# Linear attention feeding two expert stages: queries transposed beside the keys in float32, keys times values summed over pairs of units one iteration later

## The chip, the cores and the metric

The kernel runs on one core of one Trainium2 chip. The metric is the device time of one execution in microseconds; the lower the better. TensorE (PE, with its weight loads shown as PEld), VectorE (DVE), ScalarE (ACT), GpSimd (POOL) and SyncE's queue of transfers (SP) each run their own instructions in order and wait for one another through semaphores.

## The reference, cut to what matters

Batch 4, 8 heads, 576 positions, head size 64, 128 features; everything is float32.

```
phi(x): proj = x @ w_phi;  proj -= max(|proj|, over features)
        return concat(exp(proj), exp(-proj))                # 256 features
q_p, k_p = phi(q), phi(k)
kv  = sum_s k_p[s, f] * v[s, d]          # per head: 256 x 64
z   = sum_s k_p[s, f]
out = (q_p @ kv) / (q_p @ z + 1e-6)
x   = out with the heads side by side    # 2304 rows of 512
x   = top-2 mixture of 8 experts: relu(x @ w1[e]) @ w2[e], gated
y   = relu(x @ w_in)^2 @ w_out
```

## The kernel before

**Stages.** An attention loop, then eight experts of at most 640 rows each, then the dense layer. Rows go to their experts through a table in DRAM (`xg_d`) by indirect transfers that GpSimd issues (`r_5`). If an expert gets more than 640 rows, a branch at the end of the program (`tc.If(most > CAP)`) computes everything again from a copy of the attention output in `x_d`; with these inputs it is not taken, but the copy is written each time (L580, L584).

**The attention loop.** It runs n = 0 to 37. A unit is one of nine per batch: unit 0 holds the 64 tail positions of all heads, and units 1 to 8 hold 512 positions each, for keys two heads in two halves (so a pair of units makes a pair of heads), for queries one head. The order of instructions is written by hand; each step of unit u is issued in the iteration that its lag names, so in one iteration several units are at different steps. On TensorE an iteration runs, in this order:

- `k_a(n+1)`: two float32 transposes of keys into bank Tk; ACT writes the rounded high part (`kth`), DVE the low part (`ktl`).
- `q_a(n-1)`: four transposes of the query tile in float32r, high and low parts side by side, into bank Tq; ACT copies the 512 columns out (`qtr`). The high and low parts were made from the loaded tile in SBUF by `q_a0` (ACT L84, DVE L85, tile `qhl`).
- `k_b(n)`: six matmuls of key features into bank M0 or M1, then DVE's maximum (L374) and subtraction (L377).
- `q_b(n-2)`: two matmuls over 128 rows (64 of the high part, 64 of the low) and 512 columns into bank P; ACT copies them out (L473), and GpSimd takes the maximum over partitions (L475).
- `k_d(n-2)` after each second unit: eight small matmuls (`gmat`, `sel`) into Tk and a copy to `kvc`.
- `k_c(n-1)`: keys times values into bank KV, two 64-column tiles of the array at a time, then sums of the keys in four 32-column tiles (`ones`); for the first unit of a pair also the tail positions (`kpt`, from 64 rows); after the second, DVE copies the bank to `kvz` (L421), for `k_d`.
- `q_d(n-5)`: 16 matmul instructions of queries times `kvc` into N0 or N1; DVE normalizes them (`norm`) one iteration later.

Between these steps a table (`at`, `do`) hands out the rest: routing of each batch (`r_0` to `r_6`, `q_tail`), clearing of `xg_d` (`clear`), and loading and splitting the first experts' weights (`w_load`, `w_conv`). Transfers wait in SP's one queue in the order of issue.

Of the kernel before, what the change touches and what calls it, by code (L numbers as in the profile page):

```python
# [20 lines left out]
WST = 4  # L21

# [8 lines left out]
def kernel(  # L31
# [45 lines left out]
    def bank(tag, shape, dt=FT):  # L77
        return psum.tile(shape, dt, tag=tag, name=tag)
# [18 lines left out]
    LQ = [(0, 0), (0, 1), (0, 2), (1, 0), (0, 3), (1, 1), (1, 2), (1, 3)]  # L97
# [50 lines left out]
    def x_load(pt):  # L148
        e, j0, j1 = parts[pt]
        if e == E - 1:  # L150
            j1 = NJ
        src = xg_d[e * CAP:e * CAP + CAP].rearrange("(j p) d -> p j d", p=128)
        if pt == 1:
            for j in range(j0, j1):
                t = stage.tile([128, DM], FT, name="xs", tag="wstage", bufs=WST)
                nc.sync.dma_start(t, src[:, j])
                XG[pt, j] = t
        else:
            t = x_tile(pt, [128, JA if pt == 0 else NJ, DM], FT, "xg", ("qhlt", 1))
            nc.sync.dma_start(t[:, :j1], src[:, :j1])  # L160
            for j in range(j1):
                XG[pt, j] = t[:, j]

    def x_t(pt, j):
        e = parts[pt][0]
        if pt not in XT:
            n = RA if pt == 0 else CAP
            XT[pt] = (x_tile(pt, [128, DC, n], FR, "xth", ("kp", 2)), x_tile(pt, [128, DC, n], FR, "xtl", ("kp", 2)))
# [58 lines left out]
    with ExitStack() as actx:  # L227
# [28 lines left out]
        def load_tails(b):  # L256
            t = ap_.tile([TL, H, D], FT, name="ktt", tag="ktt", bufs=2)
# [7 lines left out]
            t = ap_.tile([128, 4, D], FT, name="vtt", tag="vtt", bufs=2)  # L265
            for s in range(2):
                nc.sync.dma_start(t[s * 64:(s + 1) * 64],
# [13 lines left out]
        identr = ap_.tile([128, 128], FR, name="identr", tag="identr")  # L281
# [13 lines left out]

        wf = ap_.tile([128, 128], FT, name="wf", tag="wf")
# [10 lines left out]
        jp = ap_.tile([128, 128], I32, name="jp", tag="jp")  # L307
        nc.gpsimd.iota(jp, pattern=[[1, 128]], base=0, channel_multiplier=-1)
        nc.vector.tensor_scalar(ident, jp, 0.0, None, op0=OP.is_equal)
        nc.scalar.activation(identr, ident, AF.Copy)  # L310
# [34 lines left out]
        def k_a(u):  # L345
            b, i = divmod(u, 9)
            t = bank("Tk", [128, 256])
            if i == 0:
                for p in range(4):
                    c = (p % 2 * 2 + p // 2) * 64  # L350
                    nc.tensor.transpose(t[:, c:c + 64],
                                        KTT[b][:, 2 * p:2 * p + 2, :].rearrange("p h d -> p (h d)"), ident[:64, :64])
            else:
                p, f = divmod(i - 1, 2)
                for h in range(2):
                    nc.tensor.transpose(t[:, h * 128:h * 128 + 128],  # L356
                                        KT[b, p][:, h, 2 * f:2 * f + 2, :].rearrange("p r d -> p (r d)"), ident)
            hi = ap_.tile([128, 256], FR, name="kth", tag="kth", bufs=2)
            lo = ap_.tile([128, 256], FR, name="ktl", tag="ktl", bufs=2)
            hi_lo(hi, lo, t)  # L360
            KH[u] = (hi, lo)

        def k_b(u):
# [15 lines left out]
            if i == 0:  # L379
                kp = ap_.tile([128, 4, 2, 128], FT, name="kpt", tag="kpt", bufs=1)  # L380
# [11 lines left out]
        def k_c(u):  # L392
            b, i = divmod(u, 9)
            if i == 0:
                return
            p, f = divmod(i - 1, 2)
            if f == 0:
                KVB[b, p] = bank("KV", [128, 512])
            t = KVB[b, p]
            kp = KP.pop(u).rearrange("p (h r) a f -> p r h (a f)", h=2)  # L400
            for r in range(2):
                for h in range(2):
                    mm(t[h * 64:h * 64 + 64, :256], VT[b, p][:, h, 2 * f + r, :], kp[:, r, h],
                       f == 0 and r == 0, f == 1 and r == 1)
            for h in range(2):
                for r in range(2):
                    g = 32 * (2 * h + r)
                    mm(t[g:g + 32, 256:], ones32, kp[:, r, h], False, f == 1)
            if f == 0:
                rows = slice((p // 2) * 64, (p // 2) * 64 + 64)  # L410
                kt = KPT[b].rearrange("p (r h) a f -> p r h a f", h=2)
                for h in range(2):
                    mm(t[h * 64:h * 64 + 64, :256], VTT[b][rows, (p % 2) * 2 + h, :],
                       kt[rows, p % 2, h].rearrange("p a f -> p (a f)"), False, False)
                for h in range(2):
                    for a in range(2):
                        g = 32 * (2 * h + a)
                        mm(t[g:g + 32, 256 + a * 128:384 + a * 128], ones32[rows], kt[rows, p % 2, h, a], False, False)
            else:
                kvz = ap_.tile([128, 512], FT, name="kvz", tag="kvz", bufs=1)  # L420
                nc.vector.tensor_copy(kvz, t)  # L421
                KVZ[b, p] = kvz

        def k_d(u):
            b, i = divmod(u, 9)
# [5 lines left out]
            t = bank("Tk", [128, 2, 162])  # L431
# [7 lines left out]
        QHL, QTR, PS, QP, QPT, X, XTL, LL = {}, {}, {}, {}, {}, {}, {}, {}  # L439

        def q_a0(u):
            b, i = divmod(u, 9)
            if i == 0:
                s = ap_.tile([TL, H, 2, D], FR, name="qhlt", tag="qhlt", bufs=1)
                hi_lo(s[:, :, 0, :], s[:, :, 1, :], QTT[b])
            else:
                s = ap_.tile([128, R, 2, D], FR, name="qhl", tag="qhl", bufs=2)
                hi_lo(s[:, :, 0, :], s[:, :, 1, :], QT[b, i - 1])
            QHL[u] = s

        def q_a(u):
            b, i = divmod(u, 9)
            t = bank("Tq", [128, 512], FR)
            s = QHL.pop(u)
            if i == 0:
                for h in range(H):
                    nc.tensor.transpose(t[:, h * 64:h * 64 + 64],
                                        s[:, h].rearrange("p a d -> p (a d)"), identr[:64, :64])
            else:
                for r in range(R):  # L460
                    nc.tensor.transpose(t[:, r * 128:r * 128 + 128],  # L461
                                        s[:, r].rearrange("p a d -> p (a d)"), identr)
            o = ap_.tile([128, 512], FR, name="qtr", tag="qtr", bufs=2)
            nc.scalar.activation(o, t.bitcast(FT), AF.Copy)
            QTR[u] = o

        def q_b(u):
            t = bank("P", [128, 512])
            o = QTR.pop(u)
            mm(t, wsh, o, True, False)  # L470
            mm(t, wsl, o, False, True)
            ps = ap_.tile([128, 512], FT, name="ps", tag="ps", bufs=3)
            nc.scalar.activation(ps, t, AF.Copy)  # L473
            mx = ap_.tile([128, 512], FT, name="qmx", tag="qmx", bufs=3)
# [39 lines left out]
        def q_d(u):  # L514
# [9 lines left out]
            for j in range(R):  # L524
                h = i - 1 if b < B - 1 else 2 * hp + j // 2
                for a in range(2):
                    mm(t[:, j], qp[:, a, j * 128:j * 128 + 128],
# [8 lines left out]
        def q_tail(b1, n, tag):  # L536
# [3 lines left out]
            for hh in range(4):  # L540
                h = 4 * n + hh
                for a in range(2):
                    for s in range(2):
                        mm(t[s * 64:s * 64 + 64, hh], QPT[b1 - 1 + s][:, a, h * 64:h * 64 + 64],
# [717 lines left out]
```

## Time and profile before

| what | value |
|---|---|
| median of 3 runs | 1131.83 us (1131.06 to 1132.64) |
| profiled execution | 1142.34 us, its span 1140.6 us |
| busy PE, DVE, ACT, POOL | 97%, 56%, 43%, 35% of the span |
| granted TensorE clock, mean | 0.987 |
| moved by DMA | 142.51 MB |

The profile is of one execution, longer by 10.5 us than the median of the runs. The attention loop takes its first 240 us or so; a busy share there is an average over iterations with different limits, and matmuls are pipelined, so what a matmul costs is read from the start of one group to the start of the next rather than from its own duration.

### The profile page before, as it was taken

The numbers are of one execution on the slowest core, as the hardware profiler recorded it, in microseconds if no ns is written. First come the engines' busy times: TensorE is split into PE (matmuls) and PEld (weight loads), VectorE is DVE, ScalarE is ACT, GpSimd is POOL, SyncE is SP. The second block draws the span as 40 slices with busy tenths as digits, with TensorE's granted clock in tenths as the row PEclk, the third lists the DMA queues.
The fourth block names the chain that finished last, engine by engine and source line by source line (L and its number), as shares of the span: only waits on it lengthen the run. The fifth ranks groups of instructions, "written<-read, shape, count | busy, mean of one in ns | idle before, by whom it ended". The sixth has DMA issues, their size and how long they took to land.

```text
span 1140.6 us, 17665 instructions
## 1 busy us (share of the span) xinstructions
PE 1101.5 (97%) x6588; PEld 935.0 (82%) x6588; DVE 642.7 (56%) x1247; ACT 493.8 (43%) x1025; POOL 396.8 (35%) x374
## 2 busy tenths in 40 slices
PE   7999889989999999999999999999999999999996
PEld 4676667678889999999999988888898888888885
DVE  6778778775148687878777774343343333333222
ACT  5767567641453535444445354443233232222221
POOL 3333342743545454545454545553010010000000
PEclk9999999998999999999999999999999999999998
DMA  5768352614646555555555555332112011001001
GB/s 133 223 178 263 89 168 65 208 75 173 224 142 199 180 193 183 193 178 189 179 194 180 196 182 164 122 109 74 37 39 55 19 38 56 19 1 37 1 1 40
DMA packets 106366, 142.51 MB, mean 125 GB/s; under 512 B 17570, under 2 KB 59682, under 8 KB 105762
## 3 DMA queue, kind: packets, MB, share of 16 engines
q1 hardware_dynamic: 100514, 122.44, 33.9%
q0 software_dynamic: 5760, 18.88, 5.1%
q8 instruction: 54, 0.88, 0.3%
q14 instruction: 38, 0.31, 0.1%
HBM read 92.97 MB, written 48.31 MB: 124 GB/s over the span
## 4 chain that ended last, share of the span: by engine, by line
PE 86%; DVE 6%; DMA 2%; issue 2%; ACT 1%; another core or an unknown queue 1%; POOL 1%; SPq 0%; POOLq 0%
PE M L81 38%; PE N L81 16%; PE KV L81 12%; PE P L81 9%; PE Tq L81 8%; DVE qhl L85 1%; PE Tk L81 1%; PE Tq L461 1%; PE M L173 1%; DMA wstage<-in_moe_w_dram 1%; DVE kmx L374 1%; PE Tk L995 1%; PE Tk L173 1%; PE Tk L356 1%
## 5 line engine op out<-in xcount | busy, mean ns | idle before, releaser
L1016 DVE TENSOR_TENSOR r<-M,r 128x512 f32<-128x512 f32 (+1 forms) x80 | 51.0, 638 | 245.1 <-ACT h2h L1015 242.3
L1012 ACT ACTIVATE r<-M 128x512 f32<-128x512 f32 (+1 forms) x80 | 44.4, 555 | 247.7 <-PE M L81 245.5
L202 ACT ACTIVATE hh<-M 128x320 fp32r<-128x320 f32 (+2 forms) x128 | 50.8, 437 | 227.7 <-PE M L81 220.6
L199 DVE SCALAR_TENSOR_TENSOR hl<-M,hh 128x320 fp32r<-128x320 f32 (+2 forms) x128 | 58.1, 486 | 114.7 <-ACT hh L202 113.4
L475 POOL PARTITION_ALL_REDUCE qmx<-ps x36 | 69.9, 1942 | 137.0 <-ACT ps L473 132.7
L977 POOL DMA_INDIRECT ya<-y_d,yrows x18 | 17.9, 997 | 187.2 <-PE Tk L995 112.5
L81 PEld LDWEIGHTS N<-kvc,qp 128*128 128x128 f32 x512 | 62.1, 197 | 17.5 <-issue 11.9
L81 PE MATMUL N<-kvc,qp 128*128 128x81 f32 x512 | 67.0, 284 | 9.5 <-issue 4.2
L1017 DVE TENSOR_TENSOR h2l<-r,h2h 128x512 fp32r<-128x512 f32 (+1 forms) x80 | 57.7, 721 | 7.3 <-DVE r L1016 0.5
L1015 ACT ACTIVATE h2h<-r 128x512 fp32r<-128x512 f32 (+1 forms) x80 | 47.1, 589 | 2.6
L81 PE MATMUL M<-x,w30h 128*128 128x512 f32 (+1 forms) x160 | 45.9, 371 | 0.0
L81 PE MATMUL M<-x,w20h 128*128 128x512 f32 (+1 forms) x160 | 45.7, 370 | 0.0
L81 PE MATMUL M<-x,w10h 128*128 128x512 f32 (+1 forms) x160 | 45.7, 370 | 0.0
L81 PE MATMUL M<-x,w00h 128*128 128x512 f32 (+1 forms) x160 | 45.4, 368 | 0.0
L128 POOL TENSOR_TENSOR w30l<-wstage,w30h 128x512 fp32r<-128x512 f32 x20 | 27.4, 1370 | 49.9 <-ACT w30h L127 47.4
L128 POOL TENSOR_TENSOR w20l<-wstage,w20h 128x512 fp32r<-128x512 f32 x20 | 28.0, 1399 | 45.0 <-ACT w20h L127 29.4
L740 POOL DMA_INDIRECT xg_d<-x,slots x32 | 31.9, 997 | 21.7 <-DVE slots L701 11.8
L85 DVE TENSOR_TENSOR qhl<-qt,qhl 128x256 fp32r<-128x256 f32 x32 | 37.0, 1156 | 0.4 <-ACT qhl L84 0.4
L128 POOL TENSOR_TENSOR w10l<-wstage,w10h 128x512 fp32r<-128x512 f32 x16 | 22.3, 1394 | 40.6 <-ACT w10h L127 36.8
L947 POOL TENSOR_TENSOR wd<-wd 128x256 f32<-128x256 f32 x32 | 23.7, 741 | 36.0 <-DVE wd L943 31.7
L947 POOL TENSOR_TENSOR wx<-wx 128x256 f32<-128x256 f32 x32 | 23.7, 740 | 35.1 <-DVE wx L943 31.6
L952 DVE SCALAR_TENSOR_TENSOR wd<-wd 128x256 f32<-128x256 f32 x32 | 35.1, 1096 | 1.1
(439 smaller groups left out, 3465.0 us busy)
## 6 DMA issues: line engine op xcount, KB each, us to landing
wstage<-in_moe_w_dram SPq DMA_DIRECT2D x128, 256.0 KB
xg_d<-zero SPq DMA_DIRECT2D x8, 1280.0 KB
y_d<-y SPq DMA_DIRECT2D x40, 256.0 KB
xg<-xg_d SPq DMA_DIRECT2D x7, 1280.0 KB
wide<-in_moe_w_in_dram SPq DMA_DIRECT2D x32, 256.0 KB
wide<-in_moe_w_out_dram SPq DMA_DIRECT2D x32, 256.0 KB
kt<-in_k_dram SPq DMA_DIRECT2D x16, 256.0 KB
vt<-in_v_dram SPq DMA_DIRECT2D x16, 256.0 KB
```

The costliest lines, as they stand in the source:

```text
L81: nc.tensor.matmul(o, l, r, start=start, stop=stop, skip_group_check=True)
L85: nc.vector.tensor_sub(lo, src, hi.bitcast(FT))
L128: (nc.gpsimd if n >= 2 else nc.vector).tensor_sub(lo[:, c], src, hi[:, c].bitcast(FT))
L199: nc.vector.scalar_tensor_tensor(hl[:, c0:c1], o, 0.0, hh[:, c0:c1].bitcast(FT), op0=OP.max, op1=OP.subtract)
L202: nc.scalar.activation(hh[:, c[1]:c[2]], c[0], AF.Relu)
L475: nc.gpsimd.partition_all_reduce(mx, ps, 128, bass.bass_isa.ReduceOp.absmax)
L947: nc.gpsimd.tensor_mul(part, part, exp)
L952: nc.vector.scalar_tensor_tensor(exp, ok, TINY * TINY, exp, op0=OP.is_ge, op1=OP.mult)
L1012: nc.scalar.activation(r[:, :n], t[:, :n], AF.Relu)
L1015: nc.scalar.activation(hh[:, :n], r[:, :n], AF.Square)
L1016: nc.vector.tensor_mul(r[:, :n], t[:, :n], r[:, :n])
L1017: nc.vector.tensor_sub(hl[:, :n], r[:, :n], hh[:, :n].bitcast(FT))
```

## The change

- `k_a`, `q_a0` and `q_a` become `kq_a`: the keys of unit n+1 and the queries of unit n-1 are transposed in float32 (two transposes each) into one 512-column bank, and one ACT and one DVE instruction make high and low parts of both. The tile `qhl`, the copy `qtr` and the identity `identr` go.
- `q_b`: two heads lie one above the other in the rows, so each product is taken from 64 rows: three products (high by high, high by low, low by high), each as two matmuls of 256 columns, one on the upper 64 rows into bank Tq, one on the lower 64 into bank P. The two banks become one tile, `pair`; the experts' and the dense layer's accumulators Tq and P are slices of it as well.
- `k_c` issues the values' products of both units of a pair at once. `k_c2`, an iteration later, adds the tail positions and all sums of the keys, and the bank is then copied to `kvz` by ACT, not DVE. The tails' values lie in 128 rows padded with zeros (`vtp`), the ones in `onesp`, so these matmuls use 128 rows.
- `k_d` follows an iteration later, after `k_c2`, into M0 or M1. The order of the last batch's query units changes (`LQ`).
- More buffers for `kp` and `kpt`; the weights' loads are issued two iterations earlier; the first tiles of expert 0 take their memory from `kp`.
- `x_d` is no longer written in the loop; the branch at the end gathers it from the table.

```
+PAIR = ["Tq", "P"]
...
+    pair = psum.tile([128, 2, 512], FT, tag="pair", name="pair")
+
+    def bank(tag, shape):
+        if tag not in PAIR:
+            return psum.tile(shape, FT, tag=tag, name=tag)
...
+        return pair[:, PAIR.index(tag), :n].rearrange(
...
-    LQ = [(0, 0), (0, 1), (0, 2), (1, 0), (0, 3), (1, 1), (1, 2), (1, 3)]
+    LQ = [(0, 0), (0, 1), (1, 0), (0, 2), (0, 3), (1, 1), (1, 2), (1, 3)]
...
-            t = x_tile(pt, [128, JA if pt == 0 else NJ, DM], FT, "xg", ("qhlt", 1))
+            t = x_tile(pt, [128, JA if pt == 0 else NJ, DM], FT, "xg", ("kp", 4))
...
+        vtp = [ap_.tile([128, H, D], FT, name="vtp", tag=f"vtp{i}") for i in range(2)]
+        onesp = ap_.tile([128, 2, 32], FT, name="onesp", tag="onesp")
+        for t in vtp:
+            nc.gpsimd.memset(t, 0.0)
...
-        def k_a(u):
...
+        def kq_a(n):
+            uk, uq = n + 1, n - QO + 1
...
+            t = bank("Tk", [128, 512])
...
+                    for h in range(2):
+                        nc.tensor.transpose(t[:, h * 128:h * 128 + 128],
+                                            KT[b, p][:, h, 2 * f:2 * f + 2, :].rearrange("p r d -> p (r d)"), ident)
...
+                    for f in range(2):
+                        nc.tensor.transpose(t[:, 256 + f * 128:384 + f * 128],
+                                            QT[b, i - 1][:, 2 * f:2 * f + 2, :].rearrange("p r d -> p (r d)"), ident)
+            hi = ap_.tile([128, 512], FR, name="kth", tag="kth", bufs=2)
+            lo = ap_.tile([128, 512], FR, name="ktl", tag="ktl", bufs=2)
+            c = slice(0 if has_k else 256, 512 if has_q else 256)
+            hi_lo(hi[:, c], lo[:, c], t[:, c])
...
-                kp = ap_.tile([128, 4, 2, 128], FT, name="kp", tag="kp", bufs=2)
+                kp = ap_.tile([128, 4, 2, 128], FT, name="kp", tag="kp", bufs=4)
...
         def k_c(u):
             b, i = divmod(u, 9)
+            if i == 0 or i % 2:
+                return
...
+            for f in range(2):
+                for r in range(2):
+                    for h in range(2):
+                        mm(t[h * 64:h * 64 + 64, :256], VT[b, p][:, h, 2 * f + r, :], kps[f][:, r, h],
+                           f == 0 and r == 0, False)
+
+        def k_c2(u):
...
+            for h in range(2):
+                mm(t[h * 64:h * 64 + 64, :256], VTT[b][:, 2 * p + h], kt[:, h].rearrange("p a f -> p (a f)"), False, True)
+            for f in range(2):
+                for h in range(2):
+                    for r in range(2):
+                        g = 32 * (2 * h + r)
+                        mm(t[g:g + 32, 256:], ones32, kps[f][:, r, h], False, f == 1)
             for h in range(2):
...
+                for a in range(2):
+                    g = 32 * (2 * h + a)
+                    mm(t[g:g + 32, 256 + a * 128:384 + a * 128], onesp[:, p // 2], kt[:, h, a], False, True)
+            kvz = ap_.tile([128, 512], FT, name="kvz", tag="kvz", bufs=1)
+            nc.scalar.activation(kvz, t, AF.Copy)
...
-            t = bank("Tk", [128, 2, 162])
+            t = bank(f"M{(u + 1 - 1) % 2}", [128, 2, 162])
...
-        def q_a0(u):
...
-        def q_a(u):
...
         def q_b(u):
-            t = bank("P", [128, 512])
-            o = QTR.pop(u)
-            mm(t, wsh, o, True, False)
-            mm(t, wsl, o, False, True)
+            hi, lo = QH.pop(u)
+            for i, (w, x) in enumerate(((wsh, hi), (wsl, hi), (wsh, lo))):
+                for s in range(2):
+                    rows = slice(s * 64, s * 64 + 64)
+                    mm(pair[:, s, :256], w[rows], x[rows, 256:], i == 0, i == 2)
...
-            if r + G >= R:
-                nc.sync.dma_start(_ap(x_d, b * S * DM, [[R * DM, 128], [1, R * DM]]), X[b].rearrange("p r d -> p (r d)"))
...
-            at(6 + 2 * m, 9, w_load, n, i, c)
+            at(4 + 2 * m, 9, w_load, n, i, c)
...
-            if n + 1 < NU:
-                k_a(n + 1)
...
+            kq_a(n)
             if n < NU:
                 k_b(n)
...
-            if 0 <= n - 2 < NU:
-                k_d(n - 2)
...
             if 0 <= n - 1 < NU:
                 k_c(n - 1)
+
+            if n <= NU:
+                k_c2(n - 2 if n < NU else n - 1)
+            if n <= NU + 1:
+                k_d(n - 3 if n <= NU else n - 2)
             if 0 <= n - QC < NU:
                 q_d(n - QC)
```

## Rows read from the trace of the kernel before

**Rows 1.** Busy us by stretch: PE, PEld, DVE, ACT, POOL, then granted clock, DMA share, GB/s.

```profile
80.00:90.00 10.00, 7.50 (x67) 5.34 (x68) 5.60 (x14) 5.23 (x12) 2.19 (x2) 0.98 0.96 234
...
130.00:140.00 10.00, 7.41 (x70) 5.82 (x68) 6.46 (x15) 4.50 (x9) 4.77 (x5) 0.87 0.44 131
140.00:150.00 10.00, 8.71 (x84) 6.88 (x85) 5.68 (x20) 4.40 (x9) 3.73 (x5) 0.79 0.09 32
```

**Rows 2.** The same view, a stretch of the experts.

```profile
340.00:380.00 40.00, 40.00 (x230) 36.13 (x229) 30.92 (x50) 16.16 (x39) 19.79 (x17) 1.00 0.53 173
```

**Rows 3.** The chain that ended last, two of its pieces: start, us, what.

```profile
74.84 9.40 DMA wstage<-in_moe_w_dram
...
145.99 1.32 DVE qhl L85
```

**Rows 4.** TensorE's timeline, an undisturbed stretch: start, us, what, count.

```profile
40.89 0.38 PE L356 MATMUL Tk<-ident,kt 128*128 128x128 f32 x2
...
41.40 0.35 PE L81 MATMUL M<-wbh,kth 128*128 128x256 f32 x1
...
42.19 0.40 PE L81 MATMUL P<-qtr,wsh 128*128 128x512 f32 x1
...
42.76 1.08 PE L81 MATMUL KV<-kp,vt 128*64 128x256 f32 x8
43.77 0.64 PE L81 MATMUL KV<-kp,ones 128*32 128x256 f32 x8
44.34 2.01 PE L81 MATMUL N<-kvc,qp 128*128 128x81 f32 x16
46.28 0.46 PE L351 MATMUL Tk<-ident,ktt 64*128 64x64 f32 x4
46.67 0.54 PE L461 MATMUL Tq<-identr,qhl 128*128 128x128 f32 x4
...
49.28 1.08 PE L81 MATMUL KV<-kp,vt 128*64 128x256 f32 x8
...
50.86 0.65 PE L81 MATMUL KV<-kpt,vtt 64*64 64x256 f32 x4
51.44 0.42 PE L81 MATMUL KV<-kpt,ones 64*32 64x128 f32 x8
51.79 2.01 PE L81 MATMUL N<-kvc,qp 128*128 128x81 f32 x16
53.64 0.38 PE L356 MATMUL Tk<-ident,kt 128*128 128x128 f32 x2
...
59.25 0.83 PE L457 MATMUL Tq<-identr,qhlt 64*128 64x64 f32 x8
60.01 0.38 PE L81 MATMUL M<-wbh,kth 128*128 128x256 f32 x1
```

**Rows 5.** TensorE's timeline, where later batches begin, and the second batch's long wait.

```profile
110.45 0.38 PE L356 MATMUL Tk<-ident,kt 128*128 128x128 f32 x2
...
129.40 1.34 PE L81 MATMUL N<-kvc,qpt 128*64 128x81 f32 x32
...
136.83 3.09 PE L81 MATMUL N<-kvc,qp 128*128 128x81 f32 x16 [2.59 <-ACT qp L493]
...
178.70 0.38 PE L356 MATMUL Tk<-ident,kt 128*128 128x128 f32 x2
...
234.47 0.52 PE L461 MATMUL Tq<-identr,qhl 128*128 128x128 f32 x4
```

**Rows 6.** Groups by line over the span: busy us, mean ns, idle before.

```profile
L85 DVE TENSOR_TENSOR qhl<-qt,qhl 128x256 fp32r<-128x256 f32 x32 | 37.0, 1156 | 0.4 <-ACT qhl L84 0.4
...
L464 ACT ACTIVATE qtr<-Tq 128x512 fp32r<-128x512 f32 x36 | 21.4, 596 | 3.7 <-PE Tq L461 2.3 <-PE Tq L457 1.1
...
L85 DVE TENSOR_TENSOR xtl<-M,xth 128x512 fp32r<-128x512 f32 x24 | 16.6, 691 | 14.5 <-ACT xth L84 14.5
...
L421 DVE COPY kvz<-KV 128x512 f32<-128x512 f32 x16 | 10.9, 680 | 0.0
```

More of the change, by code (lines that the diff above doesn't have):

```diff
@@ L75 @@
     g_d = dram.tile([NT, E], FT, name="g_d")
-    def bank(tag, shape, dt=FT):
-        return psum.tile(shape, dt, tag=tag, name=tag)
+    pair = psum.tile([128, 2, 512], FT, tag="pair", name="pair")
+    def bank(tag, shape):
+        if tag not in PAIR:
+            return psum.tile(shape, FT, tag=tag, name=tag)
+        names = "abc"[:len(shape) - 1]
+        n = 1
+        for x in shape[1:]:
+            n *= x
+        return pair[:, PAIR.index(tag), :n].rearrange(
+            f"p ({' '.join(names)}) -> p {' '.join(names)}", **dict(zip(names, shape[1:])))
     def mm(o, l, r, start, stop):
@@ L343 @@
         KH, KP, KPT, KVB, KVZ, KVC, KE = {}, {}, {}, {}, {}, {}, []
-        def k_a(u):
[L346 to L361, printed above, removed]
+        def kq_a(n):
+            uk, uq = n + 1, n - QO + 1
+            has_k, has_q = uk < NU, 0 <= uq < NU
+            if not (has_k or has_q):
+                return
+            t = bank("Tk", [128, 512])
+            if has_k:
+                b, i = divmod(uk, 9)
+                if i == 0:
+                    for p in range(4):
+                        c = (p % 2 * 2 + p // 2) * 64
+                        nc.tensor.transpose(t[:, c:c + 64],
+                                            KTT[b][:, 2 * p:2 * p + 2, :].rearrange("p h d -> p (h d)"), ident[:64, :64])
+                else:
+                    p, f = divmod(i - 1, 2)
+                    for h in range(2):
+                        nc.tensor.transpose(t[:, h * 128:h * 128 + 128],
+                                            KT[b, p][:, h, 2 * f:2 * f + 2, :].rearrange("p r d -> p (r d)"), ident)
+            if has_q:
+                b, i = divmod(uq, 9)
+                if i == 0:
+                    for p in range(4):
+                        nc.tensor.transpose(t[:, 256 + p * 64:320 + p * 64],
+                                            QTT[b][:, 2 * p:2 * p + 2, :].rearrange("p h d -> p (h d)"), ident[:64, :64])
+                else:
+                    for f in range(2):
[5 more added lines that the diff above has]
+            hi_lo(hi[:, c], lo[:, c], t[:, c])
+            if has_k:
+                KH[uk] = (hi, lo)
+            if has_q:
+                QH[uq] = (hi, lo)
@@ L393, in k_c @@
             b, i = divmod(u, 9)
-            if i == 0:
+            if i == 0 or i % 2:
                 return
[L396 to L401, printed above, removed]
+            p = (i - 1) // 2
+            t = bank("KV", [128, 512])
+            kps = [KP.pop(u - 1 + f).rearrange("p (h r) a f -> p r h (a f)", h=2) for f in range(2)]
@@ L578, in r_0 @@
             yield
-            if r + G >= R:
-                nc.sync.dma_start(_ap(x_d, b * S * DM, [[R * DM, 128], [1, R * DM]]), X[b].rearrange("p r d -> p (r d)"))
-            if r + G > R:
-                for s in range(2):
-                    row = (b - 1 + s) * S + SM
-                    nc.sync.dma_start(x_d[row:row + TL], XTL[b][s * 64:s * 64 + 64])
         def r_1(g):
@@ L1185, in flip @@
                 return o
+            for b in range(B):
+                for r in range(R + b % 2):
+                    x = tile_([128, DM], "sx")
+                    nc.gpsimd.indirect_dma_start(
+                        out=x, out_offset=None, in_=xg_d,
+                        in_offset=bass.IndirectOffsetOnAxis(ap=slots[:, T0[b] + r, 0:1], axis=0))
+                    if r < R:
+                        nc.sync.dma_start(_ap(x_d, (b * S + r) * DM, [[R * DM, 128], [1, DM]]), x)
+                    else:
+                        for s in range(2):
+                            row = (b - 1 + s) * S + SM
+                            nc.sync.dma_start(x_d[row:row + TL], x[s * 64:s * 64 + 64])
             with tc.For_i(0, NT, 128) as row:
```

92 lines of the change are left out of this document (29 added, 63 removed).

## The prediction

> **What bounds it now.** I read the busy times by stretch first. From 340 us on TensorE is busy 40.00 us of 40 [rows 2] and the diff leaves that work as it is, so what can move is the attention loop. There TensorE is nearly always the busiest, but not full: 7.50 us of 10 from 80 us, 7.41 from 130, 8.71 from 140, and from 130 its granted clock is 0.87 and then 0.79 of full, which means part of these stretches ran at the lower of its two levels (1.2 against 2.4 GHz) [rows 1]. The chain of waits says what fills the holes: a 9.40 us transfer of weights before ScalarE's split of them, and VectorE's `qhl` [rows 3]. The reader should see two kinds of loss: instructions on TensorE that take long, and waits.
>
> The timeline of TensorE prices both [rows 4]. Starts, not durations: front of an iteration (six transposes, six key matmuls, two query matmuls) 42.76 − 40.89 = 1.87 us; a second-of-pair `k_c` 44.34 − 42.76 = 1.58; a first-of-pair one 51.79 − 49.28 = 2.51; the pair of iterations 53.64 − 40.89 = 12.75, of which 0.25 is the tail keys' transposes (46.67 − 46.28 = 0.39 against some 0.14). A batch without waits is four pairs, 4 × 12.5 = 50.0, a ninth front 1.87, and tails of 0.25 and about 0.4 (eight transposes take 60.01 − 59.25 = 0.76, four some 0.38): 52.5 us. The batches that begin at 53.64, 110.45 and 178.70 took 56.8, 68.2 and 55.8 us [rows 4, 5]. The second also has two `q_tail` of 1.34 [rows 5]. So waits and the low clock cost 4.3, 13.0 and 3.3: 20.6 us. Of the second's 13.0, (0.13 + 0.21) × 10 = 3.4 us are clock not granted in the 20 us of rows 1 alone.
>
> **Transposes.** Six instructions become four per unit. Six take 41.40 − 40.89 = 0.51 us [rows 4], so two fewer save between 0.17 (all alike) and nothing (float32 ones slower by as much); I take 0.07, since the float32 pair is the slower kind there. Times 36 that is −2.5. The tails' eight become four: 0.76 − 0.39, four times, −1.5. Sum −4.0 us.
>
> **Query matmuls.** Two of 512 columns take 42.76 − 42.19 = 0.57, the change of array tile before KV included. Now six of 256 columns from 64 rows. A key matmul of 256 columns takes (42.19 − 41.40) / 6 = 0.13. If the upper and lower 64 rows work at once, 3 × 0.13 = 0.39; if one after the other, 0.79. To that comes entering a new tile shape. Its price follows from the sums: eight `ones` instructions of 256 columns take 44.34 − 43.77 = 0.57, eight of 128 columns 51.79 − 51.44 = 0.35; half the columns save 0.22, so 0.44 is work and 0.13 the change of shape. The values agree: 43.77 − 42.76 = 1.01 for eight, 51.44 − 50.86 = 0.58 for four, which is 0.44 per four and 0.14 once [rows 4]. So `q_b` costs 0.39 + 0.13 + 0.05 (the old group's own change of shape was in its 0.57 too) = 0.57 to 0.97: nothing to +0.40 per unit. No row splits the array by rows. The nearest split it by columns, and there tiles do work at once: eight 32-column instructions take 0.57 and eight 64-column ones 1.01. I take a third of the way, +0.13, for six loads of weights instead of two: 36 × 0.13 = +4.7 us, ends 0 and +14.4.
>
> The Trainium skill, TensorEngine Tiling (Array Packing), section Key Properties, says that changing the tiling mode drains TensorE and that tiles of one mode load and multiply in parallel; the 0.13 in rows 4 agrees with the drain, and no row here shows row tiles. By that rule alone `q_b` would stay at 0.57 and the total would be 4.7 us lower, 1109 us.
>
> **Keys times values.** A pair costs 1.58 + 2.51 = 4.09 us in six groups, each with its change of shape [rows 4]. Afterwards: 16 value instructions 1.76 + 0.13; an iteration later four for the tails 0.44 + 0.13, then sixteen `ones` 0.88 and eight tail `ones` 0.22 in one shape + 0.13. Sum 3.69, −0.40 per pair, 16 pairs: −6.4 us. Padding to 128 rows adds no column. `k_d` is only moved: nothing, covered by `q_d`'s 53.64 − 51.79 = 1.85 us between it and the next `k_b` in the same M bank; ACT's copy would have to be later than that to show.
>
> **Waits.** Per unit VectorE loses `qhl` (1.156 us, 32 of them; its `kvz` copies of 0.680 go to ACT) and its low part grows to the 512-column form, 0.691 [rows 6]: about −1.2 us per iteration, just ahead of `norm`, for which `q_d` waits through its bank. ACT loses `qtr`, 0.596, and `qhl`'s high part and gains 16 copies to `kvz` and a wider `kth`: less than before, so nothing is charged. In the second batch's long wait (2.59 us, then the low clock: 3.09 for 16 instructions that take 1.85 elsewhere [rows 4, 5]) VectorE still has two `norm` in a row, so I expect 1.2 of the 2.59 back there, and mostly the clock with it. Of 13.0 I take 8 back, of the third batch's 3.3 two. Weights are asked for three iterations before their split and not one; three iterations are 17 us against the 9.40 [rows 3], and the 4.7 MB of `x_d` leave the queue: of the first batch's 4.3 I take three. What is queued behind SP's waits comes no later: `load_q` now waits for a transpose of the same iteration instead of the split one iteration before, but its tile is used an iteration later too. Sum −13 us; the ends are −4 (VectorE was not the cause) and −18.
>
> **New waits.** At n = 34, 36 and 37 `q_d` uses a `kvc` that `k_d` makes in the same iteration (before: 35 and 37); each costs one ACT copy and its semaphores, 0.5 to 1.2 us; at 36 the copy of `kvz` is queued ahead on ACT. I charge +1. The memsets of `vtp` come ahead of the first identity on GpSimd, well under the 6 us that the first keys need to land: nothing.
>
> **Sum.** −4.0 + 4.7 − 6.4 − 13 + 1 = −17.7 us. The profiled execution has 1142.3 us, so 1124.6 there; the runs' median is 10.5 us lower, I carry the difference over whole, and predict 1131.8 − 17.7 = 1114 us.
>
> **Rivals.** (a) The row halves run one after the other: `q_b` at +0.40, 36 × 0.27 = 9.7 more, 1124 us. For it: no row shows halves working at once; against: column tiles do. The Trainium skill, TensorE: Matmul & The Clock Gate, section LDWEIGHTS, has a load cost by its columns whatever its rows; by its figure six loads are about 0.64 us, an estimate, so `q_b` would be near 0.77 and the total near 1117. No row here shows loads of two row halves.
>
> (b) The waits stay: what holds `q_d` is the chain from matmul through maximum, subtraction and `norm` and not VectorE's load, and only 4 of the 20.6 come back: 1123 us. For it: VectorE is busy only 6.46 and 5.68 us of 10 in the worst stretches [rows 1].
>
> (c) The other side: going from the upper to the lower rows empties the array each time. Then `q_b` is 0.79 for the work and 6 × 0.13 for six changes, some 1.57 us, +1.0 per unit, 36 us instead of 4.7: 1146 us. Without `q_b` the sum is −22.4, so it decides from +0.62 per unit. Against it: two 64-column tiles alternate in `KV` at 1.01 per eight with no such price.
>
> (d) Tq and P in one tile make an accumulator in one wait for the copy out of the other. The experts and the dense layer have 13 such ends; at some 0.6 to 1.2 us of copying each, 8 to 16 us: 1126 us. Against it: the two are separate banks and separate slices.
>
> (e) Both terms at their good ends, `q_b` free and 18 us of waits gone: 1104 us.
>
> **Chances.** The sum as it stands 0.52 (own range 1108 to 1120), (a) 0.15, (b) 0.14, (c) 0.08, (d) 0.05, (e) 0.06. A measurement of this kernel can tell about 0.2%, 2.3 us, from no change. Faster by more: all of the first, (e), nearly all of (a), (b) and half of (d): 0.87. Within: the tops of (a), (b) and (d) together, 0.05. Slower: (c), 0.08. The range leaves out (c) and half of (e), with a little of (d): 1104 to 1128.
>
> **What would show it.** In the new profile: the loop's batches near 48 to 51 us and evenly long; the step from the first `pair` matmul to the next group near 0.7 us (0.6: free halves; 1.0: rival a; 1.6: rival c); values in groups of 16 over 1.9 us; VectorE's `qhl` gone and its busy time lower by some 40 us; the granted clock at 1.00 from 130 to 160 us; no 9 us wait for weights near 75 us; the experts' stage as full as before. I am wrong if `q_b` is long, if TensorE's waits stay where they are, or if a wait appears at `pair` after 300 us.

## Result and profile after

The changed kernel takes 1144.57 us (median of 6 runs, 1138.43 to 1146.01), the kernel before, run beside it, 1132.32 us (1131.06 to 1133.86): ratio 1.0094, 95% interval 1.0072 to 1.0117. It is slower by 12.3 us where 17.7 us less were forecast, and outside the forecast's range. Its six runs lie in two groups, two at 1138 to 1139 us and four at 1144 to 1146, for which no cause was found; both are slower than the kernel before.

The profiled execution of the changed kernel took 1144.62 us, its span is 1142.8. The kernel before was profiled a second time among the experiments (1132.29 us, span 1130.4), and that profile is the one to compare with: the first one holds some 9 us more between the loop and the second expert, which the last section comes to. TensorE's timeline gives the places where the two part. After (start, us, what, count):

```profile
50.69 0.36 PE L92 MATMUL M<-wbh,kth 128*128 128x256 f32 x1
...
101.33 0.36 PE L92 MATMUL M<-wbh,kth 128*128 128x256 f32 x1
...
165.73 0.36 PE L92 MATMUL M<-wbh,kth 128*128 128x256 f32 x1
...
205.75 0.36 PE L92 MATMUL M<-wbh,kth 128*128 128x256 f32 x1
...
243.29 0.66 PE L184 MATMUL Tk<-ident,xg 128*128 128x128 f32 x4
...
310.77 0.57 PE L92 MATMUL M<-xth,w20h 128*128 128x320 f32 x2 [0.70 <-DVE xtl L96]
...
1131.53 0.39 PE L92 MATMUL N<-w31h,h2l 128*128 128x512 f32 x1
```

The same places in the second profile of the kernel before:

```profile
53.72 0.35 PE L81 MATMUL M<-wbh,kth 128*128 128x256 f32 x1
...
110.57 0.35 PE L81 MATMUL M<-wbh,kth 128*128 128x256 f32 x1
...
178.87 0.35 PE L81 MATMUL M<-wbh,kth 128*128 128x256 f32 x1
...
221.80 0.35 PE L81 MATMUL M<-wbh,kth 128*128 128x256 f32 x1
...
246.57 0.66 PE L173 MATMUL Tk<-ident,xg 128*128 128x128 f32 x4
...
313.34 0.56 PE L81 MATMUL M<-xth,w20h 128*128 128x320 f32 x2 [0.70 <-DVE xtl L85]
...
1120.97 0.39 PE L81 MATMUL N<-w31h,h2l 128*128 128x512 f32 x1
```

The first four rows are the first key matmul of n = 9, 18, 27 and 34; then come the first transpose of expert rows, the first product of 320 columns (the second expert), and the last product. Differences of the starts make the account:

| stretch | before, us | after, us | change, us | forecast, us |
|---|---|---|---|---|
| start to n = 34 | 221.80 | 205.75 | −16.05 | −18.7 |
| n = 34 to first transpose of expert rows | 24.77 | 37.54 | +12.77 | +1 |
| to the second expert | 66.77 | 67.48 | +0.71 | 0 |
| experts and dense layer, to the last product | 807.63 | 820.76 | +13.13 | 0 |
| last product to the end of the span | 9.43 | 11.27 | +1.84 | 0 |
| span | 1130.4 | 1142.8 | +12.4 | −17.7 |

The gain up to n = 34 looks nearly as forecast, and three stretches that the forecast held at +1 in all gave back 28 us. Part of that gain is only moved, though: `k_c2` and `k_d` run an iteration later, so behind n = 34 there still follow two whole pairs of values and sums and three `k_d`, and before the change one and a half pairs and two. TensorE from n = 34 to the first transpose of expert rows, busy by engine and granted clock, after and then in the second profile of before:

```profile
205.75:243.29 37.54, 33.61 (x307) 28.63 (x305) 22.39 (x77) 17.54 (x38) 16.07 (x18) 0.82 0.14 52
221.80:246.57 24.77, 24.24 (x258) 19.52 (x258) 22.12 (x72) 15.50 (x34) 10.69 (x9) 1.00 0.14 50
```

By these rows the +12.77 come apart. TensorE idles 37.54 − 33.61 = 3.93 us and not 0.53, which is +3.4. The clock that was not granted is (1 − 0.82) × 37.54 = 6.8 us, an estimate, against none before. The 2.6 us that are left are the moved work, and have to be taken off the gain up to n = 34.

**An undisturbed pair of iterations** after, TensorE's timeline, to be read against [rows 4]:

```profile
38.08 0.38 PE L380 MATMUL Tk<-ident,kt 128*128 128x128 f32 x2
...
38.43 0.36 PE L92 MATMUL M<-wbh,kth 128*128 128x256 f32 x1
...
39.31 0.39 PE L92 MATMUL pair<-kth,wsh 64*128 64x256 f32 x2
39.54 0.28 PE L92 MATMUL pair<-kth,wsl 64*128 64x256 f32 x2
39.65 0.28 PE L92 MATMUL pair<-ktl,wsh 64*128 64x256 f32 x2
39.86 1.95 PE L92 MATMUL KV<-kp,vt 128*64 128x256 f32 x16
41.74 0.54 PE L92 MATMUL M<-gmat,kvz 128*128 128x162 f32 x2
...
46.69 0.65 PE L92 MATMUL KV<-kpt,vtp 128*64 128x256 f32 x4
...
48.49 2.01 PE L92 MATMUL N<-kvc,qp 128*128 128x81 f32 x16
50.34 0.38 PE L380 MATMUL Tk<-ident,kt 128*128 128x128 f32 x2
```

Each `pair` line holds two matmuls with one start: the row halves work at once, and `q_b` takes 39.86 − 39.31 = 0.55 us. Four transposes take 0.35 us; the six key matmuls now take 0.88 and not 0.79, since a change of tile shape follows them. A pair's keys times values take 1.88 + (48.49 − 46.69) = 3.68 us. The pair of iterations takes 50.34 − 38.08 = 12.26 us against 12.75.

**The stretches of [rows 1, 2]** after, busy by engine, granted clock, DMA share, GB/s:

```profile
80.00:90.00 10.00, 9.95 (x98) 7.53 (x96) 6.61 (x14) 7.03 (x14) 3.88 (x2) 1.00 1.03 265
130.00:140.00 10.00, 7.46 (x85) 5.97 (x85) 5.45 (x19) 3.86 (x7) 4.32 (x6) 0.83 0.40 127
140.00:150.00 10.00, 9.96 (x71) 7.91 (x70) 4.18 (x9) 4.85 (x10) 4.78 (x6) 0.83 0.48 148
...
340.00:380.00 40.00, 38.55 (x223) 34.56 (x222) 28.49 (x47) 19.67 (x45) 18.48 (x17) 1.00 0.59 197
```

The first batch is now full (9.95 of 10). The second is not: 7.46 of 10 at a clock of 0.83. And the experts, full before, have lost 1.45 us in 40. What they wait for, after, TensorE from 285 us on (waited for: us in total, times, longest):

```profile
PE pair L92 <- ACT y L220: 8.7, 6, 1.5
PE pair L92 <- ACT o L1051: 1.0, 2, 0.5
```

No such line stands in the same view of the kernel before. One of them in the timeline of all engines:

```profile
367.13 0.40 PE L92 MATMUL pair<-w31h,hl 128*128 128x512 f32 x1
...
367.82 0.40 PE L92 MATMUL KV<-w31h,hl 128*128 128x512 f32 x1
...
369.04 0.58 ACT L220 ACTIVATE y<-pair 128x512 f32<-128x512 f32 x1
...
369.67 0.50 PE L92 MATMUL pair<-w31h,hh 128*128 128x512 f32 x1 [1.46 <-ACT y L220]
```

The first `pair` is accumulator Tq, finished some 0.4 us after 367.13. The last is P, another bank. It starts when ScalarE's copy out of Tq ends, 1.46 us after TensorE was free, and ScalarE comes to that copy only behind other work (splits of weights and the conversion of `wd`).

### The profile page after: what moved, and what is told of

It reads as the page before. It is cut to its first block, busy times and chain, and to the rows that moved or that the text cites. A ratio compares the mean times of both kernels' runs of the same rounds, so it can differ in the third digit from the quotient of the medians.

```text
span 1142.8 us, 17636 instructions
## 1 busy us (share of the span) xinstructions
PE 1096.6 (96%) x6652; PEld 940.4 (82%) x6652; DVE 606.0 (53%) x1197; ACT 478.3 (42%) x970; POOL 397.8 (35%) x379
## 4 chain that ended last, share of the span: by engine, by line
PE 72%; ACT 2%; DVE 1%; DMA 1%; issue 0%; ACTq 0%
PE M L92 36%; PE pair L92 15%; PE N L92 12%; PE KV L92 8%; PE M L184 1%; PE Tk L1010 1%; PE Tk L184 1%; DMA xg_d<-xt,slots 0%; ACT y L220 0%; DMA xs<-xg_d 0%; DVE xtl L96 0%; ACT r L1027 0%; ACT w30h L138 0%; ACT w10h L138 0%; ACT o L1051 0%
## 5 line engine op out<-in xcount | busy, mean ns | idle before, releaser
L96 DVE TENSOR_TENSOR ktl<-Tk,kth 128x512 fp32r<-128x512 f32 (+1 forms) x38 | 25.2, 663 | 54.9 <-ACT kth L95 54.9
```

## Experiments

Each time stands beside runs of the kernel before on the same chip.

**1. Two tiles instead of the pair.** The changed kernel, Tq and P as tiles of their own again; the row halves' results are copied out by two ACT instructions.

```
-    pair = psum.tile([128, 2, 512], FT, tag="pair", name="pair")
...
+            tt = [bank("Tq", [128, 256]), bank("P", [128, 256])]
...
-                    mm(pair[:, s, :256], w[rows], x[rows, 256:], i == 0, i == 2)
+                    mm(tt[s], w[rows], x[rows, 256:], i == 0, i == 2)
...
+            for s in range(2):
+                nc.scalar.activation(ps[:, s * 256:s * 256 + 256], tt[s], AF.Copy)
```

> The changed kernel with Tq and P as two tiles again; q_b's result is copied out by two ScalarE instructions of 256 columns, one for each bank. All else as changed. Theory 1 (the one tile makes an accumulator in one bank wait for the copy out of the other): the 13 us that the trace of the changed kernel loses between 276 us and its end come back, about 1131 us, and no matmul of the experts waits for the copy y. Theory 2 (the loss lies elsewhere, in the order of the last stages or in the transfers): 1143 to 1146 us, and the wait only changes its name.

Measured: 1130.13 us, before 1132.78; ratio 0.9972 (0.9954 to 0.9989). From the second expert's first product to the last product of the program 807.7 us and not 820.8, start to start. Its own waits from 285 us on are the two small ones that the kernel before has as well:

```profile
PE M L81 <- DVE xtl L85: 0.7, 1, 0.7
PE Tq L81 <- DVE h2l L1023: 0.7, 1, 0.7
```

Theory 1 holds. The rest of the change is therefore a small gain, and the pair tile turned it into a loss.

**2. The pair tile alone**, put into the kernel before; all else as there.

```
+    pair = psum.tile([128, 2, 512], FT, tag="pair", name="pair")
...
-            t = bank("Tq", [128, 512], FR)
+            t = bank("Tq", [128, 512]).bitcast(FR)
```

> The kernel before, with Tq and P as slices of one tile and nothing else changed. Theory 1: the experts and the dense layer lose about 13 us, and in the loop the query matmuls into P now wait for the copy out of Tq of the same iteration, up to 0.3 us for each of 36 units: 1145 to 1156 us. Theory 2: 1132 us, since it moves no work.

Measured: 1149.25 us; ratio 1.014 (1.0113 to 1.0167), some 16 us. Its waits from 285 us on are those of the changed kernel, 8.7 us in 6 and 1.0 in 2, and experts and dense layer take 820.7 us. The other 3.4 us lie ahead of them: the first transpose of expert rows comes 2.5 us later than in the second profile of the kernel before, the second expert another 1.0.

**3. The kernel before, profiled again.**

> The kernel before once more, unchanged, for a second profile: its first profiled execution was 10.5 us above the median of its runs. If the stretch of 249 to 258 us, where TensorE's matmuls came at 0.7 us each, is peculiar to that execution, it is absent here and the loop ends some 7 to 10 us sooner, so that most of the lead of the changed kernel at the first expert is no gain; if it belongs to the kernel, it is here again.

Measured: 1132.29 us, span 1130.4. The slow stretch is absent: from the first transpose of expert rows to the second expert it takes 66.8 us and not 75.9. This is the second profile used above.

**4 and 5. When the sums follow.** Base is experiment 1. In 4 the last batch alone, in 5 every batch issues `k_c2` in the iteration of `k_c`, and `k_d` one iteration later. Shown is 4; in 5 there is no `z`, and the earlier order holds throughout.

```
+            z = n > 29
             if n <= NU:
-                k_c2(n - 2 if n < NU else n - 1)
+                k_c2(n - 1 if z else n - 2)
             if n <= NU + 1:
-                k_d(n - 3 if n <= NU else n - 2)
+                k_d(n - 2 if z else n - 3)
```

> Base is the version with two tiles (1130.1 us). In the last batch alone the sums of keys times values and their transposes are issued one iteration earlier, so that only the last query step (n = 37) uses a kvc of its own iteration. Theory 1 (the drain of the loop lost its 7 to 9 us because at n = 34, 36 and 37 the query step waits for a kvc that is copied in the same iteration, and because the clock falls behind those waits): n = 34 takes about 5.3 us and not 9.29, the stretch from n = 35 to the first transpose of x is 2 to 3 us shorter, and the kernel takes about 1123 us. Rival (the drain is a chain of query, maximum and norm of fixed length, and a wait taken away at n = 34 comes back at 35 to 37): 1128 to 1131 us, with a PE wait for something else than kvc of the same size.

> As the run before, but in all four batches: the sums follow the values in the same iteration, the transposes follow one iteration later. It tells whether 'an iteration later' is worth anything. If the gain of keys times values is all in the order of the instructions (fewer changes of shape), batches 1 to 3 take as long as in the version with two tiles (n9 49.8, n18 100.4, n27 166.4 us) and the kernel takes the 1123 us of the run before. Rival: the later iteration is what removes a wait (for the exponentials of the second unit, or for the copy of kvz on ScalarE before its transposes): the loop loses 0.3 to 0.6 us per pair, 4 to 8 us in all, and the kernel takes 1127 to 1131 us.

Measured: 4 takes 1122.78 us, before 1133.45; ratio 0.9904 (0.9885 to 0.9924). 5 takes 1131.56, ratio 0.9985 (0.9974 to 0.9996). What 4 takes away is seen in the changed kernel's timeline of TensorE at n = 34, 36 and 37:

```profile
211.51 3.04 PE L92 MATMUL N<-kvc,qp 128*128 128x81 f32 x16 [1.30 <-ACT kvc L488]
...
226.74 2.01 PE L92 MATMUL N<-kvc,qp 128*128 128x81 f32 x16 [1.02 <-ACT kvc L488]
...
232.00 3.05 PE L92 MATMUL N<-kvc,qp 128*128 128x81 f32 x16 [1.61 <-ACT kvc L488]
```

Sixteen instructions that last 2.01 us at full clock last 3.04 behind two of the three waits: the granted clock is half from 212.3 to 215.7 and from 232.7 to 242.9 us. In experiment 4 one such wait is left, at n = 37:

```profile
229.05 2.57 PE L81 MATMUL N<-kvc,qp 128*128 128x81 f32 x16 [1.66 <-ACT kvc L477]
```

From n = 34 to the first transpose of expert rows it takes 237.17 − 208.08 = 29.1 us, against 242.46 − 206.48 = 36.0 in experiment 1: 6.9 us. Experiment 4 reaches n = 34 1.6 us later, as one `k_d` and a wait of 0.57 us now lie ahead of it, so the traces give 5.3 us in all. The medians, from two chips, are 7.4 apart. In that stretch TensorE's idle time falls from 3.97 to 1.66 us and the granted clock rises from 0.86 to 0.94, so theory 1 holds, though n = 34 takes 7.0 us and not the 5.3 that it named.

Experiment 5 answers its question against my first guess. The undisturbed pair is a little shorter without the later iteration (12.13 against 12.26 us, n = 7 to n = 9) and the batch from n = 9 to 18 is as long (50.6 us in both), but the kernel loses 8.8 us to experiment 4, a little more than the rival had: the second batch takes 67.4 and not 64.5 us, the last one 50.3 and not 48.3 up to n = 35. What grows is the wait of `q_d` for the routing's `runs`, at n = 20 and 29: 3.01 and 2.52 us, against 1.8 and 1.3 in experiment 4. So the later iteration is worth having where the loop waits, and costs in the last batch. How much is less sure. Experiments 1, 4, 7 and 8 have the same instructions from n = 18 to 27 but for the writes of `x_d`, and take 65.9, 64.5, 61.3 and 61.4 us there, at granted clocks of 0.90, 0.92, 0.97 and 0.97.

**6. The query's exponentials behind the split**, base experiment 1: `kq_a(n)` is issued ahead of `q_c2` and `q_c1`.

> Base is the version with two tiles. The two exponentials of the query (q_c2) and the subtraction before them (q_c1) are issued behind the transposes and their split instead of ahead of them, so that on ScalarE kth comes about 1.1 us and on VectorE ktl about 0.7 us earlier in a late iteration. Theory 1 (the waits of n = 20 to 22 are the chain Tk, kth behind the exponentials, ktl, maximum, subtraction, norm, and then q_d): the waits of 1.46 to 2.6 us there go, and with them the low clock of 117 to 144 us; n27 comes at 157 to 161 us and not 166.4, the kernel takes 1121 to 1125 us. Rival (q_d waits for the exponentials as much as for the norm, so that what kth gains qp loses): n27 within 2 us of 166.4, or later, with PE waits for ACT qp; 1129 to 1134 us.

Measured: 1134.24 us, ratio 1.001 (0.9995 to 1.0026), 4.1 us more than experiment 1; n = 27 begins at 167.8 us. The theory fell: TensorE's two waits for `ll` at n = 21 and 22 are 4.9 us in all, against 4.1 in experiment 1. Time and n = 27 came about as the rival had them, but the wait for `qp` that it named does not stand in the trace, so its reason is not shown.

**7. `x_d` in the loop again**, base experiment 1: the writes of `r_0` as before, no gather in the branch.

```
+            if r + G >= R:
+                nc.sync.dma_start(_ap(x_d, b * S * DM, [[R * DM, 128], [1, R * DM]]), X[b].rearrange("p r d -> p (r d)"))
...
-                    nc.gpsimd.indirect_dma_start(
-                        out=x, out_offset=None, in_=xg_d,
```

> Base is the version with two tiles. x_d is written in the loop as in the kernel before, and the gather of its rows is taken out of the branch that is not entered. Theory 1 (the larger branch costs about 2 us at the end, and the transfers of x_d in the loop collide with little): from the last matmul to the end of the span 8.9 to 9.0 us and not 11.0, the loop as long as before within 1 us, the kernel 1128 us. Rival (the transfers of 4.7 MB delay the weights and keys of the first and second batch, as they did before): n9 later by 2 to 4 us, the end shorter by 2, the kernel 1130 to 1132 us.

Measured: 1128.25 us, ratio 0.9956 (0.994 to 0.9972). The last product starts at 1115.19 of a span of 1124.6 us: 9.4 us to the end, as in the kernel before, and not 11.3. All runs with the gather in the branch take 11.3 to 11.4 us there, all without it 9.3 to 9.5. So the larger branch costs 1.9 us though it is never entered, and the 4.7 MB that it was to save the loop cost it nothing that shows: 1.9 us less in all by the medians.

**8 and 9. Together.** 8 joins experiments 1, 4 and 7; 9 adds that in the second batch VectorE normalizes the tail first, whose bank the next `q_d` reuses.

```
-            ND.append(norm(t, XTL[b1][:, n * 256:n * 256 + 256]...
+            ND.insert(0 if b1 == 1 else len(ND), norm(t, XTL[b1][:, n * 256:n * 256 + 256]...
```

> Three parts of the change undone or mended together: two tiles for the row halves (as in the first run), the last batch's sums an iteration earlier (1122.8 us with the first), and x_d written in the loop, with no gather in the branch that is not entered (1128.3 us with the first). If the three losses are separate, they add: 1130.1 - 7.4 - 1.9 = 1120.8 us, ratio 0.989. Rival (the drain and the x_d transfers meet in the last batch's loads, so that one gain hides the other): 1122.5 to 1124 us.

> As the run with the two parts undone, and in the second batch the norm of a tail is issued on VectorE ahead of the norm of the query step that was issued before it, since the next query step reuses the tail's N bank. Theory (the long iterations n = 21 and 22 are one serial chain: tail on TensorE, transposes, kth, ktl, maximum, difference, two norms, query step; VectorE's load does not matter, only what stands on this chain): the waits of 1.48 and 2.59 us ahead of the query steps at n = 21 and 22 shrink by 0.87 us each, perhaps with a little low clock, and the kernel gains 1.5 to 3 us over the run beside it. Rival (the norms are not what is late; N is released by something else, or the clock sets the length): n = 21 and 22 as long as before within 0.3 us, no gain.

Measured: 8 takes 1122.23 us, ratio 0.9907 (0.9885 to 0.993); 9 takes 1118.77, ratio 0.9868 (0.9849 to 0.9887), the fastest version here, 14.5 us under the 1133.28 of the kernel before beside it. 8 is no faster than experiment 4 by its ratio (0.9904): that the 7.4 us of the last batch and the 1.9 of the branch add up is not shown, though its last stretch is 9.5 us as in experiment 7. For 9, first the changed kernel's waits of n = 20 to 22:

```profile
118.22 1.98 PE L92 MATMUL N<-kvc,qp 128*128 128x81 f32 x16 [1.74 <-DVE runs L692]
...
128.22 1.98 PE L92 MATMUL N<-kvc,qp 128*128 128x81 f32 x16 [1.46 <-DVE ll L538]
...
139.24 2.45 PE L92 MATMUL N<-kvc,qp 128*128 128x81 f32 x16 [2.54 <-DVE ll L538]
```

And VectorE ahead of the last of them:

```profile
134.12 0.69 DVE L96 TENSOR_TENSOR ktl<-Tk,kth 128x512 fp32r<-128x512 f32 x1 [4.81 <-ACT kth L95]
134.73 0.68 DVE L416 TENSOR_REDUCE kmx<-M 128x4 f32<-128x512 f32 x1
135.45 0.69 DVE L419 TENSOR_TENSOR kd<-M,kmx 128x512 f32<-128x512 f32 x1
...
137.00 0.66 DVE L536 TENSOR_TENSOR x<-N,rec 128x256 f32<-128x256 f32 x1
...
138.83 0.27 DVE L538 TENSOR_TENSOR ll<-N,rec 128x64 f32<-128x64 f32 x1
```

VectorE idles 4.81 us before this chain begins; it is not loaded, it is waited for. Transposes, `kth`, `ktl`, key matmuls, maximum, difference and two norms stand in a row, and `q_d` at the end. In experiment 9 the same two waits, at n = 21 and 22:

```profile
126.95 1.98 PE L81 MATMUL N<-kvc,qp 128*128 128x81 f32 x16 [0.51 <-DVE den L517]
135.40 2.29 PE L81 MATMUL N<-kvc,qp 128*128 128x81 f32 x16 [1.53 <-DVE den L517]
```

Experiment 8 has 1.48 and 2.59 us there, so each shrank by about 1 us, as the theory of the chain has it. The time did not follow in the traces. From n = 18 to 27 TensorE's idle time falls from 5.90 to 3.87 us, but the granted clock from 0.97 to 0.94, and the stretch is only 0.4 us shorter (60.95 and 61.36). The two profiled spans differ by 0.7 us (1117.5 and 1116.8), the medians by 3.5 with intervals that touch: the waits are shown, the gain in time is not sure.

**10. The query part alone** in the kernel before, with two tiles. The wider buffers and the earlier loads of weights stay in as well.

> The kernel before with the query part alone: queries in float32 beside the keys, one split for both, three products from row halves into two tiles; keys times values, their sums, the transposes of kv in Tk and x_d as in the kernel before. Theory 1 (the row halves work at once, so that the query part is worth the two transposes and the small difference of q_b, and VectorE's and ScalarE's smaller load brings little because the waits are a chain): 3 to 6 us faster than before, 1127 to 1130 us, with the second batch's long iterations as they were. Rival (the query part brings most of the 10 us that the loop up to n = 27 gained, because qhl and qtr were in the way of the norms): 1121 to 1125 us. Second rival (kv in Tk now waits for the wider split, since one Tk holds keys and queries): slower than before by up to 0.5 us per pair, 1135 to 1140 us.

Measured: 1131.57 us, ratio 0.9986 (0.9965 to 1.0008), nothing that can be told from no change; theory 1 was closest but promised a little more. The second rival's wait is there, TensorE for Tk behind the wider low part, 7.1 us in 8 waits from 30 us on, and takes from the gain: the pair of n = 7 and 8 takes 5.56 + 7.46 = 13.02 us, 12.76 in the second profile of before. With kv in the M banks, as in the changed kernel, `k_d` has no such wait. TensorE's two waits for `ll` in the second batch are 2.3 us in all here, 3.9 in the kernel before and 4.0 in the changed kernel.

**11. The pair tile kept, the banks' order changed**: the changed kernel with one other line.

```
-    ACC = ["Tq", "KV", "P", "N0", "N1"]
+    ACC = ["Tq", "KV", "N0", "P", "N1"]
```

> The changed kernel, pair tile and all, with one line different: the order in which an expert's five accumulators take the banks is Tq, KV, N0, P, N1 and not Tq, KV, P, N0, N1, so that P's last product comes behind two groups of the first layer and not one accumulator behind Tq. Theory 1 (P's product waits for ScalarE's late copy out of Tq because both are slices of one tile; nothing else is wrong with the pair): the waits of 1.46 us at pair are gone, first 320-column product to last product near 808 us and not 821, the kernel 1131 to 1135 us. Rival (the pair tile costs in other ways too, at every first product of an expert or in the dense layer): the wait moves to another accumulator and the kernel stays at 1138 to 1145 us.

Measured: 1140.18 us, but on a chip where the kernel before takes 1145.61: ratio 0.9964 (0.9946 to 0.9981), against 1.0094 for the changed kernel. The waits at `pair` for a copy of `y` are gone; experts and dense layer take 808.0 us. In absolute time the expectation missed: 1140.18 lies in the rival's range, which like the theory's was written for a chip with 1132 us. Carried over by the ratio it is 0.9964 × 1132.3 = 1128 us, 3 under the theory's range, and the rival's sign, a wait that moves to another accumulator, is absent. So the tie of P to Tq in the experts was the whole loss at the pair.

## Why the prediction was wrong

**The step that failed** is the term for the experts and the dense layer, which the sum puts at nothing because "the diff leaves that work as it is". The tie of the two banks stands only as rival (d), set aside with a chance of 0.05 because "the two are separate banks and separate slices". Its mechanism was right. Experiments 1, 2 and 11 show it from three sides: the pair away, alone, and with other accumulators between its halves. Two banks that are slices of one tile behaved as one thing to wait for. Experiment 1 also speaks for the program's tracking by tile and against the memory itself: there the same accumulators lie in two banks as well, and nothing waits. How the program sets these waits was not examined. The rival's price, 8 to 16 us, holds the 13.1 that were measured, in part by luck: the rival took 13 ends at 0.6 to 1.2 us, and the profile has six waits of up to 1.5 us and two of up to 0.5, 9.7 us in all. One more wait at `pair` (0.7, for `x`) and matmuls that last longer make up the rest: TensorE is busy 809.65 us in this stretch, before 806.82. The prediction's own sign for being wrong, "a wait appears at `pair` after 300 us", is the line that the profile shows.

**New waits** were forecast at +1 us for n = 34, 36 and 37. They are 1.30, 1.02 and 1.61 us, 3.9 in all against 0.5 before; two lie above the 1.2 that was taken for the longest. The clock that falls behind them was left out, and so was that this is the end of the loop, where nothing else fills TensorE. Together these make 3.4 of idle time and some 6.8 of clock not granted, 10 of the +12.8 us; the other 2.6 are work moved from the loop. Experiment 4 takes 5.3 us back in all. The order of the last batch's query units (`LQ`) was not run alone.

**Waits, −13.** This term failed too, and the loop's total hides it. Of the 16.05 us up to n = 34, 2.6 are moved work, and about 15 pairs at 0.49 with the forecast's 1.5 for tails are 8.9 of shorter instructions. Some 4.5 us of waits came back, near the forecast's end of −4, which is rival (b); that the total came near −18.7 is luck. TensorE's own rows agree: from the first key matmul to n = 34 it idles 9.9 us, before 13.4, at a granted clock of 0.97 in both, while VectorE is busy 130.2 us and not 164.8.

The first batch gave its part: it takes 50.64 us against 56.85, of which about 2.6 are shorter instructions, so 3.6 of waits where 3 were taken. With the writes of `x_d` back in the loop (experiment 7) it takes 50.64 as well, so it was not these that had to go; the earlier loads and the wider buffers were not run alone. The second batch did not: 64.40 against 68.30, of which again about 2.6 are shorter instructions, so 1.3 where 8 were to come, and the granted clock is 0.83 from 130 to 150 us where 1.00 was to be the sign. TensorE's two waits for `ll` are 4.0 us in all as before (3.9), though `qhl` is gone. This is rival (b): the wait is a chain, and a lighter VectorE did not shorten it. `qhl` was not nothing on it, as experiment 10 has 2.3 us there; what brings the wait back in the changed kernel was not tested. The busy share of 6.46 and 5.68 [rows 1] already spoke for (b).

**Transposes, query matmuls, keys times values.** Four transposes save 0.16 us and not 0.07. The prediction took the float32 pair for the slower kind; the row between those of [rows 4] says otherwise:

```profile
41.02 0.54 PE L461 MATMUL Tq<-identr,qhl 128*128 128x128 f32 x4
```

The two float32 transposes ahead of it take 41.02 − 40.89 = 0.13 us, these four 41.40 − 41.02 = 0.38. `q_b` takes 0.55 where 0.70 were taken and 0.57 was the good end, with 0.09 more ahead of it for the change of shape; the values' and sums' 3.68 us are the forecast's 3.69. Per pair −0.49 against −0.28. Rivals (a) and (c) fell with the 0.55. "No row splits the array by rows" overlooks the `kpt` groups of [rows 4], which use 64 rows, though only one half at a time. The Trainium skill's rule that different tiles work in parallel (TensorEngine Tiling (Array Packing), Key Properties) agrees with this 0.55. The 0.77 estimated from a load's figure in the Trainium skill (TensorE: Matmul & The Clock Gate, LDWEIGHTS) does not, and the measurement decides.

**Not in the forecast at all**: the branch that is not entered, +1.8 us (experiment 7).

**What was right**: the account against the profiled execution, with its 10.5 us carried over whole. The second profile, within 0.5 us of the median, shows that those were not the kernel's.

## What to carry to other kernels

Two banks in one tile save an instruction in one place and can tie every other user of these banks together: look up who else has them, and in which order they finish and are copied. A part that makes something an iteration later helped here only where the loop waits, and costs at its end; treat the last batch apart, and take work that is merely moved behind a mark off the gain up to that mark. And before a wait is credited to an engine that gets lighter, see whether that engine idles ahead of the chain that ends the wait: if it does, look at the chain's order first.

## What was not expected of the hardware

The lower clock followed two of the three short waits at the loop's end. Ahead of 211.5 us TensorE idled 1.30 us, from 212.3 to 215.7 us the granted clock is half (1.2 and not 2.4 GHz) with TensorE busy all the time, and sixteen instructions last 3.04 and not 2.01 us. With half of these 3.4 us the wait of 1.3 costs some 3.0, an estimate. Behind the wait of 1.02 us at 226.74 the clock stayed full.

And on one chip, that of experiment 11, the kernel before takes 12 to 13 us more than on the others. The profile of experiment 11 shows one place, at the end of the loop, where TensorE's instructions come in small groups with idle time that ends with no other engine ("issue"):

```profile
250.26 0.57 PE L92 MATMUL N<-kvc,qp 128*128 128x81 f32 x4 [0.78 <-issue]
251.69 0.58 PE L92 MATMUL N<-kvc,qp 128*128 128x81 f32 x4 [0.86 <-issue]
253.16 0.55 PE L92 MATMUL N<-kvc,qp 128*128 128x81 f32 x3 [0.89 <-issue]
```

The five idle times named so are 3.2 us in all, and the granted clock from 250 to 260 us is 0.71. From the first transpose of expert rows to the second expert it takes 75.6 us there, 75.9 in the first profile of the kernel before, which shows such groups at the same place, and 66.8 in the second. Why TensorE issues so slowly there stays open.
